# Block-sparse attention in front of a top-2 mixture of experts: dense heads in split f16 against gathered key blocks in f32

## The chip, the cores and the metric

The kernel runs on one core of one Trainium2 chip. The metric is the time of one execution in device microseconds (us); the median of several executions is given where there are several. A core has five engines with queues of their own: TensorE (PE, its weight loads shown as PEld), VectorE (DVE), ScalarE (ACT), GpSimd (POOL) and SyncE (SP), which only issues DMAs. DMAs can be issued on SP's, ACT's and POOL's queues; they share 16 DMA engines. Within a queue everything goes in order, so a DMA that has to wait holds back what stands behind it.

## The reference, cut to what matters

The attention has 4 batches, 8 heads, 768 positions and 64 columns a head. The mask is by blocks of 32: a query block sees its neighbours, the first and the last key block, and three key blocks that come as input; the first and the last query block see everything.

```python
mask = np.abs(blk_i - blk_j) <= 1
mask = mask | (blk_i == 0) | (blk_j == 0) | (blk_i == n_blocks - 1) | (blk_j == n_blocks - 1)
for qb in range(n_blocks):                       # 24 blocks
    for kb in sampled_blocks[qb]:                # 3 each, an input
        mask[qb*32:(qb+1)*32, kb*32:(kb+1)*32] = True
scores = np.where(mask, scale * q @ k.T, -1e9)
attn = softmax(scores); x = attn @ v             # then (B*S, H*D) = (3072, 512)
noisy = x @ w_gate + log1p(exp(x @ w_noise)) * noise
# each row goes to its two best of 8 experts, with softmax weights over the two:
out[row] += weight * (relu(x[row] @ w1[e]) @ w2[e])       # w1: 512x1024, w2: 1024x512
```

All inputs are f32 but the block numbers, which are 64-bit integers.

## The kernel before

The program is written in the order in which each engine's queue is to run; there is no planner behind it. It has two stages.

**Attention** goes head by head, two heads a group, in 192 steps (32 heads x 6 key tiles of 128). Q, K and V are loaded on ACT's queue. Q and K are split into an f16 high and low part (`split`, ACT and POOL), and turned by DMA transposes on SP (`xpose`). The mask rides along as 24 extra columns: one-hot block numbers times 2^15 on the query side, allowed blocks on the key side. For each step PE computes a first product only for the row maxima (`max_mm`, line 214), DVE takes the maximum over 768 columns (`max_red`, line 221), the maximum is put back into the operands by another DMA transpose (line 232), PE computes the scores transposed, keys by queries, in two f16 matmuls of 384 columns (`exp`, lines 245 and 246), ACT takes the exp out of PSUM (line 247), and PE multiplies by V in f32, two column tiles at once (`av`, line 302). The row sums are added up over key tiles by POOL or DVE, whichever a running estimate of their work says is free (`plus`, line 271), summed by PE with a matrix of ones (line 313), and the result is turned back by PE (line 341), scaled by DVE (line 344) and split into f16 high and low (lines 353, 355).

**The router** (`Router.run`) is a chain of some forty small operations for each batch. It is a generator: a call of `background` lets it go one step, between the operations of attention, and for the last batch between those of the first expert. It ends in twelve indirect DMAs on POOL that write row number and weight into a table of slots, ordered by expert.

**The experts** (`Experts`) come in nine units: expert 0 for the first three batches (unit 0, 640 slots), expert 0 for the last batch (unit 1, 224 slots), and experts 1 to 7 with 816 slots. For a unit, SP loads its slots (`meta`, line 809), POOL gathers the rows (`gather`, line 836), SP turns them by DMA transpose (`xpose`, line 846), PE runs the two layers in split f16 (`mm1` line 888, `mm2` line 908), DVE multiplies by the weight and adds what is there already (`finish`, line 949), which POOL has gathered from the output before (`gather_prev`, line 854), and POOL scatters the rows to the output (line 955). Weights come in eight pieces for each expert (`load_piece`, SP, line 792) and are split into high and low f16 by ACT and DVE (`split_piece`, lines 799 and 800).

What belongs to the seam stands in the main function: a dictionary `plan` says at which attention step the router's inputs are loaded, the output is zeroed (`fill_out`, line 1078, eight DMAs on ACT's queue from step 20 on), the first weight pieces are loaded, and slots, gathers and transposes of unit 0 are issued, in the last 14 steps.

Of the kernel before, what the change touches and what calls it, by code (L numbers as in the profile page):

```python
# [18 lines left out]
P = 128  # L19
# [18 lines left out]


class Attention:  # L40
    G = 2
    XM = 2
    RN = 5
    S0 = 4
    Q2LATE = 1
    ROWLATE = 2
    LOADAT = 2
    VLOADAT = 6

    SPLITAT = ((0, 0, 0), (1, 0, 1), (2, 1, 0), (5, 1, 1), (5, 2, None), (6, 3, None), (8, 4, None), (9, 5, None))  # L50
    PPB = 5
    STEP = 2000
    AHEAD = 4000
    SPARE = 2000
    LA = 4

    def __init__(self, tc, q, k, v, sampled):
        self.tc, self.nc = tc, tc.nc
        self.q, self.k, self.v, self.sampled = q, k, v, sampled
        self.B, self.H, self.S, self.D = q.shape  # L60
        self.T = self.S // P
        self.NB = self.S // 32
        self.LM = self.T + 5
        self.NG = self.B * self.H // self.G
        self.NSTEP = self.B * self.H * self.T
        self.st = {}
        self.todo = {}
        self.now = 0
        self.busy = {"v": 0.0, "p": 0.0, "a": 0.0}

    def open(self, ctx, early):

        tc, nc, G, T = self.tc, self.nc, self.G, self.T
        pool = lambda c, name, bufs, **kw: c.enter_context(tc.tile_pool(name=name, bufs=bufs, **kw))
        self.const = pool(ctx, "aconst", 1, side="right")
        self.tp = pool(ctx, "atp", 3, side="right")
        self.pp = pool(ctx, "app", self.PPB, side="right")
        self.sm = pool(ctx, "asm", 4, side="right")
        self.xp = pool(ctx, "axp", 2, side="right")
        self.ps_e = pool(ctx, "ps_e", 3, space=PSUM)  # L80
        self.ps_m = pool(ctx, "ps_m", 2, space=PSUM)
        self.ps_o = pool(ctx, "ps_o", 1, space=PSUM)
        self.natp = pool(ctx, "anat", 1, side="right")
        self.raw = pool(early, "araw", 2)
        self.nat = [tuple(self.natp.tile([P, G, T, P], F16, name=f"{n}{i}") for n in ("ka", "qa", "qb"))
                    for i in range(2)]
        self.k2 = [self.natp.tile([P, G, T, P], F16, name=f"k2{i}") for i in range(3)]
        self.vx = [self.natp.tile([P, G, T, self.D], F32, name=f"vx{i}") for i in range(3)]

        self.inv = self.natp.tile([P, 32], F32, name="inv")  # L90
        nc.gpsimd.memset(self.inv, 1.0 / XS)
        self.ident = self.natp.tile([P, P], F32, name="ident")

    def masks(self, mi, sb):

        nc, T, NB, G = self.nc, self.T, self.NB, self.G
        BIG = 2.0 ** 15
        bc = lambda a, n: a[:, None, :].to_broadcast([P, T, n])
        rowi = mi.tile([P, T], I32, name="rowi")
        nc.gpsimd.iota(rowi, pattern=[[1, T]], base=0, channel_multiplier=T)  # L100
        ei = mi.tile([P, NB], F32, name="ei")
        nc.gpsimd.iota(ei, pattern=[[1, NB]], base=0, channel_multiplier=0,
                       allow_small_or_imprecise_dtypes=True)
        self.kb = mi.tile([P, G, T, P], F16, name="kb")
        nc.gpsimd.memset(self.kb[:, :, :, 64:], 0.0)
        nc.gpsimd.memset(self.kb[:, :, :, 64 + NB:65 + NB], 64.0)
        self.blank(0)
        nc.vector.tensor_scalar(rowi, rowi, 5, None, op0=ALU.arith_shift_right)
        rowb = mi.tile([P, T], F32, name="rowb")
        nc.vector.tensor_copy(rowb, rowi)  # L110
        rb = rowb[:, :, None].to_broadcast([P, T, NB])
        eh = mi.tile([P, T, NB], F32, name="eh")
        nc.vector.tensor_tensor(eh, bc(ei, NB), rb, op=ALU.is_equal)
        self.eh = eh
        self.blocks(0, 1)
        t1 = mi.tile([P, T, NB], F32, name="t1")
        nc.vector.tensor_tensor(t1, bc(ei, NB), rb, op=ALU.subtract)
        al = mi.tile([P, T, NB], F32, name="al")
        nc.vector.tensor_tensor(al, t1, t1, op=ALU.mult)
        nc.vector.tensor_scalar(al, al, 1.5, None, op0=ALU.is_lt)  # L120
        e0 = mi.tile([P, NB], F32, name="e0")
        nc.vector.memset(e0, 0.0)
        nc.vector.memset(e0[:, 0:1], 1.0)
        nc.vector.memset(e0[:, NB - 1:NB], 1.0)
        nc.vector.tensor_tensor(al, al, bc(e0, NB), op=ALU.add)
        nc.vector.tensor_tensor(al, al, eh[:, :, 0:1].to_broadcast([P, T, NB]), op=ALU.add)
        nc.vector.tensor_tensor(al, al, eh[:, :, NB - 1:NB].to_broadcast([P, T, NB]), op=ALU.add)
        sbf = mi.tile([P, 3, NB], F32, name="sbf")
        nc.vector.tensor_copy(sbf.rearrange("p j e -> p e j"), sb.rearrange("p (e j) k -> p e j k", j=3)[:, :, :, 0])
        t3 = mi.tile([P, T, 3, NB], F32, name="t3")  # L130
        nc.vector.tensor_tensor(t3, sbf[:, None].to_broadcast([P, T, 3, NB]),
                                rowb[:, :, None, None].to_broadcast([P, T, 3, NB]), op=ALU.is_equal)
        for j in range(3):
            nc.vector.tensor_tensor(al, al, t3[:, :, j], op=ALU.add)
        for g in range(G):
            nc.vector.tensor_scalar(self.kb[:, g, :, 64:64 + NB], al, 0.0, -BIG, op0=ALU.is_equal, op1=ALU.mult)

    def blank(self, i):
        ka, qa, qb = self.nat[i]
        self.nc.gpsimd.memset(qa[:, :, :, 64 + self.NB:], 0.0)  # L140
        self.nc.gpsimd.memset(qb[:, :, :, 64 + self.NB:], 0.0)

    def blocks(self, i, k):
        for g in range(self.G):
            self.nc.vector.tensor_scalar(self.nat[i][k][:, g, :, 64:64 + self.NB], self.eh, 2.0 ** 15, None, op0=ALU.mult)

    def load(self, g, eng=None, names="kq"):
        b, h0 = divmod(g * self.G, self.H)
        r = self.st.setdefault(g, {})
        for nm in names:  # L150
            if nm == "v":
                x = r["v"] = self.vx[g % 3]
                (eng or self.nc.scalar).dma_start(x.rearrange("p h t d -> p h (t d)"),
                                                  self.v[b, h0:h0 + self.G].rearrange("h (p t) d -> p h (t d)", p=P))
                continue
# [5 lines left out]
    def new(self, r, nm):  # L161
        r[nm] = self.tp.tile([P, self.G, self.T, P], F16, name=nm)
        return r[nm]
# [34 lines left out]
    def where(self, n):  # L198
        hh, i = divmod(n, self.T)
        g, h = divmod(hh, self.G)  # L200
        return g, h, i
# [1030 lines left out]
```

## Time and profile before

| | us |
|---|---|
| median of 3 runs (lowest, highest) | 1067.92 (1065.22, 1068.31) |
| span of the profiled execution, first to last instruction | 1027.3 |
| attention: start to the first expert matmul | 438.3 |
| experts: from there to the last matmul's output | 572.4 |
| tail | 16.6 |
| PE busy in the span | 952.4 |
| DVE, ACT, POOL busy in the span | 506.3, 374.4, 518.5 |

The profile is of one execution. Its own time is not listed apart from its span; the median of the runs is 40.6 us above the span, which is what lies around the first and last instruction. In the rows of groups the columns are line, engine, operation, tiles written <- read, shapes and count; then the busy time of the group, the mean ns of one, the engine's idle time just before them, and what ended it. Names such as `po<-p,vx` are the program's own tile names. Matmuls overlap in the pipeline, so a group's count times its mean is more than its busy time; an f32 matmul shows as two records.

### The profile page before, as it was taken

Reading aid. Unit: us, or ns where it says so; the run is one execution under the profiler, and the core shown is the slowest. Engines: PE = TensorE matmul, PEld = TensorE weight load, DVE = VectorE, ACT = ScalarE, POOL = GpSimd, SP = SyncE. Lnnn points to the kernel's source line nnn. Section 1 sums busy time; section 2 is a strip of 40 time slices with the busy share of each in tenths; the row PEclk is TensorE's granted clock in tenths of the full one; section 3 lists DMA queues with packets and bytes.
Section 4 is the critical chain, followed back from the end, with each engine's and each line's share of the span. In section 5 each row is a group of like instructions: output and inputs, shape, how many; then the busy total and the mean of one; then the engine's idle time right before and its main releaser. Section 6 shows DMA issues by size and latency. Waiting matters only on the chain. (4 is left out here: it accounts for less than half of the span.)

```text
span 1027.3 us, 14952 instructions
## 1 busy us (share of the span) xinstructions
PE 952.4 (93%) x5633; PEld 452.3 (44%) x5633; DVE 506.3 (49%) x845; ACT 374.4 (36%) x795; POOL 518.5 (50%) x488
## 2 busy tenths in 40 slices
PE   3999999999999989789779999999999999989993
PEld 1344343444344434265545455454454544544541
DVE  6666669876887776165414425134143341341220
ACT  2566656565566645443203124032031230320200
POOL 2687886887688758925434142151342512612111
PEclk9999999999999989999889999999999999999997
DMA  8899975787577647655588539269295393681200
GB/s 193 187 183 274 250 185 112 156 163 161 128 154 153 122 100 130 134 165 122 151 219 205 185 109 257 82 159 227 73 219 156 116 220 112 152 173 56 61 34 33
DMA packets 238499, 156.04 MB, mean 152 GB/s; under 512 B 173025, under 2 KB 214241, under 8 KB 238416
## 3 DMA queue, kind: packets, MB, share of 16 engines
q1 hardware_dynamic: 207264, 91.45, 42.1%
q0 software_dynamic: 14256, 39.58, 13.3%
q10 hardware_dynamic: 16896, 23.95, 8.5%
q8 instruction: 46, 0.75, 0.3%
q14 instruction: 37, 0.30, 0.1%
HBM read 79.62 MB, written 26.32 MB: 103 GB/s over the span
## 5 line engine op out<-in xcount | busy, mean ns | idle before, releaser
L247 ACT ACTIVATE p<-pe 128x384 f32<-128x384 f32 x384 | 186.9, 491 | 154.9 <-PE pe L246 136.5
L221 DVE TENSOR_REDUCE m<-pm 128x1 f32<-128x768 f32 x192 | 182.2, 953 | 93.6 <-PE pm L214 92.1
L955 POOL DMA_INDIRECT out_dram<-y,mt x56 | 60.5, 1081 | 315.2 <-DVE y L949 211.5
L893 ACT ACTIVATE hh<-ph 128x408 f16<-128x408 f32 (+2 forms) x136 | 66.6, 490 | 340.6 <-PE ph L888 280.9
L302 PE MATMUL po<-p,vx 128*64 128x384 f32 x768 | 160.7, 511 | 0.0
L271 POOL TENSOR_TENSOR acc<-p,p 128x768 f32<-128x768 f32 x69 | 125.0, 1812 | 26.6 <-ACT p L247 26.4
L894 DVE SCALAR_TENSOR_TENSOR hl<-ph,hh 128x408 f16<-128x408 f32 (+2 forms) x136 | 76.0, 560 | 125.9 <-ACT hh L893 125.9
L245 PE MATMUL pe<-q,k 128*128 128x384 f16 x384 | 129.1, 336 | 6.5 <-DVE xr L344 3.7
L246 PE MATMUL pe<-q,k 128*128 128x384 f16 x384 | 126.5, 329 | 3.3 <-DMA q<-qb 3.3
L949 DVE SCALAR_TENSOR_TENSOR y<-py,mt,pv 128x512 f32<-128x512 f32 (+1 forms) x55 | 41.2, 749 | 168.1 <-PE py L908 150.5
L888 PE MATMUL ph<-xta,w1hb 128*128 128x408 f16 x512 | 111.2, 340 | 10.1 <-DMA xta<-xg 6.4
L908 PEld LDWEIGHTS <-hh 128*128 128x128 f16 x768 | 75.0, 98 | 98.4 <-issue 10.4
L214 PE MATMUL pm<-k,q 88*128 88x384 f16 x384 | 98.4, 341 | 18.4 <-DMA k<-kb 10.7
L888 PE MATMUL ph<-xtb,w1ha 128*128 128x408 f16 (+1 forms) x448 | 91.2, 325 | 2.9 <-DVE hl L894 2.4
L245 PEld LDWEIGHTS <-k 128*128 128x128 f16 x384 | 37.1, 97 | 118.5 <-issue 105.2
L271 POOL TENSOR_TENSOR acc<-acc 128x768 f32<-128x768 f32 x41 | 74.2, 1811 | 19.8 <-DVE acc L274 17.0
L908 PE MATMUL py<-w2ha,hh 128*128 128x512 f16 x192 | 73.8, 384 | 5.9 <-DVE y L949 5.4
L854 POOL DMA_INDIRECT pv<-out_dram,gi x56 | 57.8, 1031 | 34.5 <-issue 17.8
L908 PE MATMUL py<-w2ha,hl 128*128 128x512 f16 x192 | 73.6, 383 | 0.7 <-DVE hl L894 0.7
L908 PE MATMUL py<-w2la,hh 128*128 128x512 f16 x192 | 73.8, 384 | 0.0
L888 PEld LDWEIGHTS <-w1ha 128*128 128x128 f16 x576 | 56.4, 98 | 39.4 <-issue 3.9
L908 PE MATMUL py<-w2hb,hh 128*128 128x512 f16 x192 | 72.8, 379 | 0.4 <-DVE y L949 0.3
(179 smaller groups left out, 1306.6 us busy)
## 6 DMA issues: line engine op xcount, KB each, us to landing
wraw<-in_moe_w_dram SPq DMA_DIRECT2D x64, 512.0 KB, 5.8
q<-q SPq DMA_DIRECT2D x32, 192.0 KB, 3.3
vx<-in_v_dram ACTq DMA_DIRECT2D x16, 384.0 KB, 4.1
out_dram<-zero ACTq DMA_DIRECT2D x8, 768.0 KB, 5.2
x_rows<-x SPq DMA_DIRECT2D x16, 384.0 KB, 3.5
raw_k<-in_k_dram ACTq DMA_DIRECT2D x14, 384.0 KB, 4.1
raw_q<-in_q_dram ACTq DMA_DIRECT2D x14, 384.0 KB, 5.9
k<-k SPq DMA_DIRECT2D x17, 192.0 KB, 4.5
```

The costliest lines, as they stand in the source:

```text
L214: self.nc.tensor.matmul(pm[:, c, 0:384], r["q3"][0:K, h, t, :], r["k2"][0:K, h, 3 * c:3 * c + 3, :], start=True, stop=True)
L221: self.nc.vector.tensor_reduce(self.st[g]["m", h][:, t:t + 1], pm[:, :, 0:384], axis=AX.XY, op=ALU.max)
L245: nc.tensor.matmul(pe[:, 0:384], r["k1"][:, h, c, :], r["q1"][:, h, t, :], start=True, stop=False)
L246: nc.tensor.matmul(pe[:, 0:384], r["k2"][:, h, c, :], r["q2", h][:, t, :], start=False, stop=True)
L247: nc.scalar.activation(p32[:, t].rearrange("p t c -> p (t c)"), pe[:, 0:384], AF.Exp, scale=0.125)
L271: self.nc.gpsimd.tensor_add(out, a, b)
L302: self.nc.tensor.matmul(po[s * D:(s + 1) * D], r["v"][:, h, c, :], p32[:, 3 * s:3 * s + 3].rearrange("p t c -> p (t c)"), start=c == 0, st ...
L888: nc.tensor.matmul(ph[:, b, 0:m], w[wt][:, kb, fs], r["xt"][:, kb, a, o:o + m], start=i == 0, stop=i == last)
L893: nc.scalar.activation(hv, ph[:, b, 0:m], AF.Relu)
L894: nc.vector.scalar_tensor_tensor(self.hl[:, f, o:o + m], ph[:, b, 0:m], 0.0, hv, op0=ALU.max, op1=ALU.subtract)
L908: nc.tensor.matmul(py, h[:, f, o], w[x][:, f, :], start=i == 0, stop=i == last)
L955: nc.gpsimd.indirect_dma_start(out=self.out, out_offset=bass.IndirectOffsetOnAxis(ap=r["mt"][0:m, c, 0:1], axis=0), in_=y[0:m], in_offset= ...
```

## The change

- The host part of the launch lays Q and K out as [64 columns x 2 heads, positions] in f32 and puts the first and last query block of a batch together at the end; V gets a column of ones for each head and 32 rows of zeros at the end. So no DMA transposes and no f16 splits of Q and K, no mask columns, and no separate row sums are left in attention.
- A batch has six query tiles of 128: five of four ordinary blocks (`g` 0 to 4), and one special tile (`SPEC`) with the ordinary blocks 21 and 22 and the full blocks 0 and 23, which see all keys. Its work is 16 macros: per half of the heads D, D, X for the special tile (D: the two full blocks against 384 keys each; X: blocks 21 and 22), then G for each of the five ordinary tiles and each half.
- In a G or X, a query block has 256 key columns: 160 gathered ones (three sampled blocks, first and last block, in `KG`) and 96 that are next to each other in `KT`. POOL copies the sampled blocks of K at offsets read into registers (`gather_k`). SP loads V twice over: `VA` with the three sampled blocks, each by a DMA of its own at a register offset, and the first block; `VB` with the last block and the three neighbours (`load_v`). A sampled block that is there already, or twice, gets the zero rows of V.
- PE's score matmuls are 32 or 64 queries wide, 64 rows deep, in tiles of the array (`scores`); DVE takes the maximum from PSUM (`top`), ACT the exp (`exps`), PE turns the result in f32 (`turn`), ACT and DVE copy it out of PSUM (`evac`), PE multiplies by V and its column of ones (`av`), DVE divides (`norm`), ACT and POOL split into f16 (`high`, `low`).
- The steps run three deep: at step n the scores of macro n, the turn of n - 1, the AV of n - 2.
- Everything that attention and router load goes on SP's queue. Row stores are per tile, and the noise and row numbers follow the new order of rows (32 small DMAs for the noise).
- `fill_out` goes from attention into the first layer of unit 0, still on ACT's queue; `zero` becomes a tile of its own. Units 0 and 1 no longer read the output before they write it.
- Slots, gathers and transposes of unit 0 are issued after attention's last step, and the tiles that they write are opened there. Weight pieces 0 to 3 of expert 0 are issued in the last eight steps, as before in the last 22.
- The bookkeeping of engine work (`work`, `plus`) goes.

The diff, cut to its core:

```diff
+    def load_v(self, b, g):
+        ...
+        if self.seq(b, g) == i:
+            nc.sync.dma_start(VA[96:P], at(row, 32, [[0, 4]]))
+            nc.sync.dma_start(VB[0:32], at(row + self.S - 32, 32, [[0, 4]]))
+        ...
+        nc.sync.dma_start(VB[32:P, ks[0]:ks[0] + len(ks)], at(row + 32 * (f + ks[0] - 1), 96, [[32 * width, len(ks)]]))
+        ...
+        _, offs = nc.values_load_multi_w_load_instructions(
+            self.voff[0:1, b, 3 * f:3 * (f + n)], engines=(mybir.EngineType.SP,), min_val=0, max_val=self.ZROW,
+            skip_runtime_bounds_check_because="block numbers")
+        for j in range(n):
+            for s in range(3):
+                nc.sync.dma_start(VA[32 * s:32 * s + 32, j], v[bass.ds(offs[3 * j + s], 32)])
+    def gather_k(self, b, g):
+        ...
+        for j in range(n):
+            for s in range(3):
+                nc.gpsimd.tensor_copy(KG[:, j, :, 32 * s:32 * s + 32], KT[:, :, bass.ds(offs[3 * j + s], 32)])
+    def scores(self, m):
+        ...
+        mm = lambda out, l, r, pos: nc.tensor.matmul(out, l, r, start=True, stop=True, tile_position=pos)
+        ...
+        for some in tiles:
+            for piece in range(2):
+                for r, j, o, col in some:
+                    for a in range(2):
+                        ...
+                        mm(S[a][o:o + 32, sl], q[hp(a), pr, 32 * j:32 * j + 32], rhs, (64 * a, o))
+    def steps(self, on_tile, step):
+        ...
+        for n in range(NS + 3):
+            new, mid, old = at(n), at(n - 1), at(n - 2)
+            if old:
+                self.evac(old, 0)
+                self.evac(old, 1)
+            if new:
+                self.scores(new)
+            step(n, 0)
+            if new:
+                self.top(new)
+            if new:
+                self.exps(new)
+            step(n, 1)
+            if old:
+                self.av(old)
+                self.norm(old)
+            if mid:
+                self.turn(mid)
+            step(n, 2)
+            if old:
+                self.high(old)
+                self.low(old, on_tile)
+            if new:
+                self.ahead(n)
+            step(n, 3)
...
-        nc.vector.scalar_tensor_tensor(y[0:m], py[0:m, 0:self.D], r["mt"].bitcast(F32)[0:m, c, 1:2], self.pv[0:m, c, :],
-                                       op0=ALU.mult, op1=ALU.add)
+        if u < 2:
+            nc.vector.tensor_scalar(y[0:m], py[0:m, 0:self.D], w[0:m, c, 1:2], None, op0=ALU.mult)
+        else:
...
-    at(NS - AHEAD, ex.meta, 0)
-    for c in range(ex.count(0)):
-        at(NS - AHEAD + 2 + c // 2, gather_early, c)
-        at(NS - AHEAD + 4 + c // 2, ex.xpose, 0, c)
...
-    for i in range(8):
-        at(20 + 4 * i, fill_out, i)
+    OPEN = NS - 8
...
     att.steps(on_tile, step)
+    while not finished(B - 2):
+        background()
     late.close()
+    ex.open_left(left)
     ex.open_right(right)
+    ex.meta(0)
+    ex.indices(0)
+    for c in range(ex.count(0)):
+        ex.gather(0, c)
+    for c in range(ex.count(0)):
+        ex.xpose(0, c)
...
-    ex.gather_prev(0)
...
             if u == 0:
+                fill_out(f)
                 for i in SPLITS[f]:
                     ex.split_piece(0, i)
```

More of the change, by code (lines that the diff above doesn't have):

```diff
@@ L87, in open @@
[L87 to L136, printed above, removed]
@@ L249, in flush @@
-    def flush(self):
-        for n in sorted(self.todo):
-            for f in self.todo.pop(n):
-                f()
-    def later(self, steps, f):
-        if steps:
-            self.todo.setdefault(self.now + steps, []).append(f)
-        else:
-            f()
-    def work(self, v=0, p=0, a=0):
-        for e, x in (("v", v), ("p", p), ("a", a)):
-            self.busy[e] += x
-    def plus(self, out, a, b):
-        u, w = self.busy["v"] + 1050, self.busy["p"] + 1800
-        if out is a and min(u, w) > self.now * self.STEP - self.SPARE:
-            return False
-        if w <= u:
-            self.nc.gpsimd.tensor_add(out, a, b)
-            self.work(p=1800)
-        else:
-            self.nc.vector.tensor_add(out, a, b)
-            self.work(v=1050)
-        return True
@@ new lines, in turn @@
+    def turn(self, m):
+        kind, b, g, h, kh = m
+        p = self.st.pop(("p", m))
+        T = self.st["tp", m] = [self.ps_t.tile([P, 512], F32, name=f"t{a}") for a in range(1 if kind == "X" else 2)]
+        if kind == "D":
+            src = [(a, k, 384 * a + P * k) for a in range(2) for k in range(3)]
+        elif kind == "X":
+            src = [(0, 2 * c + u, 256 * u + P * c) for c in range(2) for u in range(2)]
+        else:
+            src = [(c, u, 256 * u + P * c) for c in range(2) for u in range(4)]
+        for t, i, o in src:
+            self.nc.tensor.transpose(T[t][:, i * P:(i + 1) * P], p[:, o:o + P], self.ident)
@@ new lines, in start, with ahead @@
+    def start(self, ip):
+        self.load_q(0, self.SPEC)
+        self.load_k(0)
+        self.index(ip)
+        self.load_vn(0)
+        make_identity(self.nc, self.ident)
+        self.gather_k(0, self.SPEC)
+        self.load_v(0, self.SPEC)
+        for g in range(2):
+            self.load_q(0, g)
+            self.load_v(0, g)
+        self.gather_k(0, 0)
+    def ahead(self, n):
+        b, i = divmod(n, self.PB)
+        order = [(bb, g) for bb in (b, b + 1) for g in (self.SPEC, *range(self.SPEC))]
+        more = b + 1 < self.B
+        last = not more
+        if i == 3 and more:
+            self.load_k(b + 1)
+        if i == 7 and more:
+            self.load_vn(b + 1)
+        unit = lambda k: order[k] if order[k][0] < self.B else None
+        qs = {6: 3, 8: 4, 10: 5, 12: 6, 14: 7} | ({0: 2} if b else {})
+        vs = {7: 3, 9: 4, 11: 5, 13: 6, 15: 7} | ({1: 2} if b else {})
+        if last:
+            vs = {7: 2, 9: 3, 11: 4, 13: 5}
+        ks = {5: 2, 7: 3, 9: 4, 11: 5, 13: 6, 15: 7}
+        for plan, f in ((ks, self.gather_k), (qs, self.load_q), (vs, self.load_v)):
+            if i in plan and (u := unit(plan[i])):
+                f(*u)
@@ L561, in run @@
         nc.vector.tensor_copy(lc, pv)
-        work(v=325)
         yield
@@ L589, in run @@
         nc.vector.reciprocal(iw, w)
-        work(v=250)
         yield
```

719 lines of the change are left out of this document (333 added, 386 removed).

## The prediction

> **What bounds the kernel now.** I read the page first (engine sums, then the groups), then three stretches of the span, then TensorE's instructions in order of time, then the queues. The first fence has the engine sums and the costly groups of attention from the page; the second has the stretches: attention, experts, tail, each row with its length and then the busy time of PE, PEld, DVE, ACT and POOL, the granted clock and the DMA share.
>
> ```profile
> PE 952.4 (93%) x5633; PEld 452.3 (44%) x5633; DVE 506.3 (49%) x845; ACT 374.4 (36%) x795; POOL 518.5 (50%) x488
> L247 ACT ACTIVATE p<-pe 128x384 f32<-128x384 f32 x384 | 186.9, 491 | 154.9 <-PE pe L246 136.5
> L221 DVE TENSOR_REDUCE m<-pm 128x1 f32<-128x768 f32 x192 | 182.2, 953 | 93.6 <-PE pm L214 92.1
> ```
>
> ```profile
> 0.00:438.30 438.30, 402.23 (x2525) 164.78 (x2525) 301.75 (x508) 245.91 (x591) 333.36 (x300) 0.99 0.76 163
> 438.30:1010.70 572.40, 550.18 (x3108) 287.56 (x3108) 203.76 (x336) 128.46 (x205) 184.12 (x187) 0.99 0.57 147
> 1010.70:1027.30 16.60, 0.00 (x0) 0.00 (x0) 0.75 (x1) 0.00 (x0) 0.98 (x1) 0.62 0.05 19
> ```
>
> PE is busy 402 of 438.3 us in attention and 550 of 572.4 in the experts, and the others wait for it (ACT 136.5 us and DVE 92.1 us of idle time end on a matmul). So attention is a PE stage. The change takes three quarters of its score work away; what counts is which resource then sets the 438.3 us, and what the seam to the experts costs. Around the span lies 1067.9 (median) - 1027.3 = 40.6 us, which I keep; the profiled execution has no time of its own listed, so the sum goes by its span and is then put on the median.
>
> **PE after the change.** f32 matmuls in column tiles, the f32 transposes and the seam, in order of time:
>
> ```profile
> 251.83 0.87 PE L302 MATMUL po<-p,vx 128*64 128x384 f32 x4
> 252.63 0.19 PE L554 MATMUL pe<-r_whl,r_xT 128*128 128x32 f16 x1
> 255.80 0.53 PE L313 MATMUL pe<-acc,inv 128*32 128x192 f32 x8
> 256.27 0.34 PE L245 MATMUL pe<-q,k 128*128 128x384 f16 x1
> 436.47 0.55 PE L341 MATMUL pe<-ident,xo 128*128 128x128 f32 x3
> 438.32 0.71 PE L888 MATMUL ph<-xta,w1ha 128*128 128x320 f16 x2 [1.30 <-DVE xr L344]
> ```
>
> Two column tiles of 384 f32 columns take 252.63 - 251.83 = 0.80 us, four of 192 take 0.47: each f32 column costs 2.1 to 2.4 ns, however many tiles share it. Transposes follow each other every (0.55 - 0.27)/2 = 0.14 us, 0.27 being the length of one. The new attention has 64 macros (16 a batch): 40 of kind G (four query blocks, four heads), 16 D, 8 X. A G has 2 x (160 + 96) = 512 score columns in eight tiles: 1.2 us; eight transposes: 1.1; AV in eight groups of four tiles of 65 columns: 1.25. That is 3.55. A pair of D: 2 x (0.8 + 6 x 0.14) + 12 x 65 x 2.4 ns = 5.2; an X: 1.8. Sum 142 + 42 + 14 = **198 us**. No row shows tiles that split the rows of the array too: if those two run one after the other, scores double and PE has about 265; if the short pieces overlap better it has 180. I take 198, since the column tiles do share.
>
> **DVE, ACT and the chain of a step.** Rows for what replaces the old work:
>
> ```profile
> L344 DVE TENSOR_TENSOR xr<-pe,rc 128x384 f32<-128x384 f32 x32 | 17.6, 549 | 2.1 <-PE pe L341 2.0
> L561 DVE COPY r_lc<-pe 128x192 f32<-128x192 f32 x3 | 1.1, 358 | 4.4 <-PE pe L556 4.4
> L949 DVE SCALAR_TENSOR_TENSOR y<-py,mt,pv 128x512 f32<-128x512 f32 x48 | 36.0, 750 | 165.4 <-PE py L908 150.5 <-DMA pv<-out_dram,gi 11.8 <-DMA slots<-r_pay,r_sl 3.1
> L336 DVE RECIPROCAL rc<-sbt 128x6 f32<-128x6 f32 x32 | 6.1, 192 | 1.1
> L274 DVE TENSOR_TENSOR acc<-p,p 128x768 f32<-128x768 f32 x27 | 28.1, 1040 | 0.0
> L274 DVE TENSOR_TENSOR acc<-acc 128x768 f32<-128x768 f32 x12 | 11.5, 955 | 0.0
> L334 DVE STREAM_TRANSPOSE sbt<-sb 128x192 f32<-128x192 f32 x32 | 11.8, 370 | 20.1 <-ACT sb L331 20.1
> L331 ACT ACTIVATE sb<-pe 128x192 f32<-128x192 f32 x32 | 10.5, 327 | 3.4 <-PE pe L313 3.4
> ```
>
> DVE in a G: two maxima over 512 (953 x 512/768 = 0.64 each), two small operations on four columns and the reciprocal (under 0.2 each), one copy of 512 out of PSUM (0.70, between 358 x 512/192 and 750), one scaling of 256 (0.37): 2.9 us. D pairs 3.3, X 1.9: 115 + 27 + 15 = 157. The maxima over 768, the sums and the rest of the old attention go. What is left of DVE's 301.75 us when the rows of lines 221, 274, 334, 336 and 344 are taken off (182.2 + 28.1 + 11.5 + 11.8 + 6.1 + 17.6), 44 us of router and start, stays: 200 us. ACT: four exps of 256 (0.38 each, from 327 for 192 and 491 for 384), a copy of 512 (0.6), half of a 512 conversion: 2.4 a G, 133 in all. Per macro the order is scores, maximum, exps, turn, evacuation, AV, spread over three steps with two score buffers: 1.2 + 1.45 + 1.5 + 1.1 = 5.25 us over two steps, so at least 2.6; PE's 3.55 is larger. With hand-overs, and the D pairs holding both score buffers until the exps, I take 4.0 a step: 64 x 4.0 = **256 us**, plus 15 for the start.
>
> **SP, the queue that gets nearly everything.** Loads that went out on ACT's queue now go on SP's, and each gathered value block is a DMA of its own, whose offset is first read into a register. First two issues in order of time, then lines with min/median/max ns of one issue; L971 is the only read of a value into a register; then the bytes of the first 438 us, all and ACT's queue.
>
> ```profile
> 1.23 0.42 SPq L368 DMA_DIRECT2D raw_k<-in_k_dram  x1
> 1.70 0.42 SPq L368 DMA_DIRECT2D raw_q<-in_q_dram  x1
> L538 SPq DMA_DIRECT2D x_rows<-x x16: 583/964/1328, 73.7 to 441.3; - x16
> L536 SPq DMA_TRANSPOSE r_xT<-x x16: 1313/1528/4252, 70.1 to 439.8; - x16
> L971 SPq TENSOR_LOAD <-o_nt x1: 472/472/472, 987.3 to 987.3; - x1
> L836 POOLq MOVE  x56: 29/29/29, 405.9 to 888.0; - x56
> DMA packets 143892, 71.54 MB, mean 163 GB/s; under 512 B 111216, under 2 KB 137328, under 8 KB 143856
> q10 hardware_dynamic: 16896, 23.95, 20.0%
> ```
>
> Counted from the code: 264 gathers (24 tiles, six of them a batch, 12 blocks each but 6 for the first); 166 other plain DMAs (8 K, 4 VN, 24 Q, 24 + 16 VB, 22 end blocks, 32 x_rows, 36 for router inputs and the table); 24 transposes; 264 register values. A plain issue repeats every 1.70 - 1.23 = 0.47 us; I take 0.5 for the 166 = 83. Transposes 24 x 1.58 = 38. A gather is a small DMA of 32 rows: 0.47 plus some register arithmetic (29 ns an instruction), 0.57, so 150; its bounds are 0.47 and the 1.01 of an average x_rows issue. A register value lies between one 472 ns load for each list of 12 (11 us in all) and 472 ns for each value (125); I take 60, the middle, because a list is one address range and most of 472 ns should be the round trip. Sum 83 + 38 + 150 + 60 = **331 us**, bounds 255 (with all low) and 512. [...] No run here shows a list yet.
>
> SP works in order. A value load waits for the AV that frees its buffer (three buffers, two in the last batch); behind it stand the next Q, the row stores and the next batch's K. The wait falls five steps before the use, so in a SP-bound stage PE is there first and it costs nothing.
>
> Bytes: the code moves 72.6 MB in attention (17.6 gathered V, about 23.4 VB and ends, 12.6 Q and K, 6.4 VN, 12.6 rows and their transposes), as much as the 71.54 before, but in runs of 2 KB. ACT's queue moved 23.95 MB of such runs in 20.0% of 438 us, 273 GB/s: 266 us, under SP's sum.
>
> **POOL.** K blocks are gathered by copies of 128 columns at a register offset:
>
> ```profile
> masks.py:199 POOL TENSOR_SCALAR_AFFINE_SELECT ident<-ident 128x128 f32<-128x128 f32 x1 | 0.3, 292 | 0.1
> L355 POOL TENSOR_TENSOR x<-xr,x 128x384 f16<-128x384 f32 x31 | 28.4, 915 | 0.2
> L716 POOL DMA_INDIRECT slots<-r_pay,r_sl x36 | 38.9, 1081 | 8.9 <-issue 5.9 <-DVE r_ot L706 2.4 <-DVE m L221 0.6
> ```
>
> 264 copies at 0.29 to 0.5 (take 0.4): 106; their values 60; 24 subtractions of 512 columns at 1.22 = 29; scatters 39; end blocks 16: 250, under SP too (172 to 342).
>
> **The seam and the experts.** First the latencies to landing (us, last number) of what fills the first expert, then min/median/max ns of an issue:
>
> ```profile
> out_dram<-zero ACTq DMA_DIRECT2D x8, 768.0 KB, 5.2
> xg<-x_rows,gi POOLq DMA_INDIRECT x56, 4.9
> xta<-xg SPq DMA_TRANSPOSE x33, 5.5
> mt<-slots SPq DMA_DIRECT2D x1, 5.0 KB, 2.8
> L809 SPq DMA_DIRECT2D mt<-slots x9: 340/530/538, 407.8 to 844.3; - x9
> L1078 ACTq DMA_DIRECT2D out_dram<-zero x8: 542/550/628, 67.4 to 123.4; - x8
> L836 POOL DMA_INDIRECT xg<-x_rows,gi x56: 923/998/1497, 411.1 to 894.5; - x56
> ```
>
> Before, slots, gathers and transposes of the first expert were issued during attention and PE idled 1.30 us. Now they follow its last step: norm, high, low about 3 us; on SP the last transpose and row store 2.6; slots 0.9 + 2.8; limits 0.4; five gathers at 1.05 on POOL, the last landing 4.9 later; its transpose 5.5: **25 us** of idle PE, 24 more than before. Loading the first weights in the last eight steps hides behind attention as before. Zeroing on ACT's queue is 8 issues of 0.55, hidden (ACT has 128 us of work in 572); its 6.3 MB meet the weights in the first unit, where the output scatters also wait for it: 5 us by estimate (0 to 20). Seven gathers of earlier output fall away on POOL, which is idle: nothing. The different DVE operation for the first two units costs the same.
>
> **Sum.** Attention is set by SP: 331, plus 5 while SP stands for the first offsets, plus about 12 from the last value load's issue to the last matmul less 8 of row work behind it: 340. First expert matmul at 365 instead of 438.3; experts 572.4 + 5; tail 16.6: span 959, and with 40.6 around it **1000 us**; the likeliest case's own range is 955 to 1045.
>
> **Rivals.**
> (1) SP is not the bound: gathers at 0.47 and lists read at once, 255 us, and then the chain of a step (256 + 15) sets attention: 271 + 25 + 577 + 17 + 41 = 931, range 905 to 955. For it: the nearest issue row; against: POOL and the DMA engines stand near 255 too.
> (2) Slower: a gathered block costs SP more than 1.06 us (issue and value together, I took 0.80). Then 264 x 0.26 = 69 us more, attention ends at 409 and the seam and zeroing eat the rest: 1068 at the turning point, 1115 at 1.24, 1180 at the upper ends (1.01 + 0.47 = 1.48). For it: x_rows at 0.96 and the only register row at 0.47; against: the 0.42 of short issues.
> (3) The clock falls. PE would be busy 198 of 340 us with gaps at each wait, and the tail's row shows 0.62 granted where PE stands still, against 0.99 in attention. At half clock for the whole stage PE has 396 us and the time is about 1055. [...]
> (4) The change doesn't shorten attention at all because the DMA engines fill: 72.6 MB at the 163 GB/s of before is 445 us, about 1110 in all. Against: that was 256-byte packets for the most part.
>
> **Chances.** Forecast 0.47, (1) 0.24, (2) 0.20, (3) 0.04, (4) 0.02, and 0.03 for an end within 0.3% of before, which is about what runs of this kernel can tell. Faster 0.75, same 0.04, slower 0.21. The range 910 to 1095 takes in (1), the forecast, (3) and the nearer part of (2), and leaves out under 2 in 10.
>
> **What would show it.** Right: attention's last matmul near 340, SP issuing back to back through it, about 0.8 us between gathers, PE busy near 200 us before the seam, 25 us of idle PE, experts within 10 us of 572. If SP shows long stands and the steps last 4 us, (1); if the gathers come every 1.1 us or more, (2); if the clock row is well under 0.9 in attention, (3). Wrong altogether would be an expert stage that grows by tens of us: PE waiting for weights or for output scatters behind the zeroing, which I priced at 5.

## The result, and the profile after

The changed kernel takes **1100.93 us** (median of 4 runs, 1097.33 to 1103.69) beside 1067.04 (1065.22 to 1068.31) for the kernel before in the same comparison: ratio **1.0317 [1.0284, 1.0351]**. I had forecast 1000 in a range of 910 to 1095. The same kernel was timed twice more beside the kernel before: 1.0247 [1.0176, 1.0317] (1058.41 us) and 1.0407 [1.0369, 1.0445] (1106.55 us). Chips differ: before takes 1033 to 1034 us in two of the five comparisons and 1064 to 1067 in three, so below only ratios, or profiles of one group of chips, are compared. I call them the quick chips (1033) and the slow chips (1066).

First the stretches of the changed kernel's profiled execution (1101.8 us, span 1100.0; slow chip): attention, seam, experts, tail; then the same two large stretches of the kernel before and of the changed kernel on quick chips. Columns: stretch, length, busy time of PE, PEld, DVE, ACT, POOL, granted clock of PE (1.00 is full), DMA share (mean busy share of the 16 DMA engines), GB/s.

```profile
0.00:456.00 456.00, 264.57 (x6761) 201.03 (x6761) 186.87 (x580) 133.62 (x310) 142.78 (x413) 0.78 0.67 166
456.00:474.60 18.60, 1.51 (x49) 1.36 (x48) 0.93 (x4) 0.63 (x1) 7.26 (x8) 0.54 0.64 155
474.60:1081.90 607.30, 560.12 (x3060) 289.49 (x3060) 204.82 (x336) 128.31 (x204) 181.03 (x178) 0.96 0.58 145
1081.90:1100.00 18.10, 0.00 (x0) 0.00 (x0) 0.75 (x1) 0.00 (x0) 0.98 (x1) 0.60 0.05 18
```

```profile
0.00:432.70 432.70, 400.54 (x2514) 164.08 (x2514) 300.39 (x505) 244.98 (x588) 330.88 (x299) 0.99 0.78 165
436.80:1012.90 576.10, 551.58 (x3108) 288.37 (x3108) 203.78 (x336) 128.20 (x205) 183.12 (x187) 0.98 0.58 146
```

```profile
0.00:439.90 439.90, 244.39 (x6758) 190.90 (x6759) 186.43 (x580) 133.95 (x310) 142.12 (x413) 0.81 0.70 172
458.50:1041.80 583.30, 553.05 (x3060) 287.24 (x3060) 204.03 (x336) 128.85 (x204) 180.97 (x178) 0.97 0.60 151
```

On quick chips the 30.0 us between the spans (1060.1 - 1030.1) are attention +7.2, seam +14.5 (18.6 for 4.1), experts +7.2 and tail +1.1. The change did what it says: PE's work in attention fell from 400.5 to 244.4 us, DVE's from 300 to 186, ACT's from 245 to 134, POOL's from 331 to 142. No engine is full any more, and yet attention isn't shorter. So the question is what each engine waits for. PE's waits in the first 456 us of the changed kernel, then those of SP's queue (us in all, times, longest):

```profile
PE pe L536 <- DMA r_xT<-x: 45.1, 6, 15.1
PE s L197 <- DMA q<-in_q_dram: 37.4, 8, 13.1
PE s L197 <- issue: 22.8, 35, 1.4
PE t L277 <- ACT p L253: 18.5, 8, 7.6
PE po L305 <- DMA va<-in_v_dram: 17.4, 11, 4.7
```

```profile
SPq L516 <- POOL x L372: 62.0, 5, 26.8
SPq L171 <- DMA vb<-in_v_dram: 12.9, 8, 3.1
SPq L144 <- PE pe L619: 12.5, 1, 12.5
```

And a batch border (where one batch's last tiles end and the next batch's scores begin) in order of time, SP's queue first, then PE:

```profile
128.76 6.23 SPq L171 DMA_DIRECT2D va<-in_v_dram  x12
135.04 0.42 SPq L144 DMA_DIRECT2D q<-in_q_dram  x1
135.57 1.29 SPq L516 DMA_TRANSPOSE r_xT<-x  x1
```

```profile
139.00 0.21 PE L536 MATMUL pe<-r_whl,r_xT 128*128 128x32 f16 x1 [14.65 <-DMA r_xT<-x]
139.52 1.56 PE L197 MATMUL s<-kt,q 64*64 64x384 f32 x8
```

The router's matmuls of a finished batch stand in PE's order ahead of the next scores. They need the last row tile's transpose; SP issues it only at 135.57, behind the twelve gathers of a value tile. PE stands 14.65 us. While PE stands no new tile is finished, and SP then stands for the next batch's first row tile, 62.0 us at five places. The two wait for each other in turn, at each of three borders. PE's second row, the wait for Q, stands on the same queue: Q too is issued behind the twelve gathers (135.04).

### The profile page after: what moved, and what is told of

Its sections match the earlier page's. It is cut to its first block, busy times and chain, and to the rows that moved or that the text cites. A ratio compares the mean times of both kernels' runs of the same rounds, so it can differ in the third digit from the quotient of the medians.

```text
span 1100.0 us, 24431 instructions
## 1 busy us (share of the span) xinstructions
PE 826.2 (75%) x9865; PEld 491.9 (45%) x9865; DVE 393.4 (36%) x921; ACT 262.6 (24%) x515; POOL 332.1 (30%) x600
## 5 line engine op out<-in xcount | busy, mean ns | idle before, releaser
L262 ACT ACTIVATE p<-s,nb 128x256 f32<-128x256 f32 x176 | 69.5, 475 | 165.2 <-DVE nb L240 77.8
L188 POOL COPY kg<-kt 128x128 f32 x264 | 64.0, 295 | 114.1 <-PE s L197 88.2
L277 PE MATMUL t<-ident,p 128*128 128x128 f32 x448 | 79.9, 328 | 23.2 <-ACT p L253 18.5
L223 DVE TENSOR_REDUCE nm<-s 128x2 f32<-128x512 f32 (+1 forms) x96 | 57.5, 641 | 111.0 <-PE s L197 102.3
L197 PE MATMUL s<-kg,q 64*32 64x160 f32 x1408 | 62.3, 360 | 46.3 <-DMA q<-in_q_dram 27.3
L197 PE MATMUL s<-kt,q 64*32 64x96 f32 (+1 forms) x1536 | 68.1, 316 | 31.4 <-issue 15.5
L305 PE MATMUL po<-va,t 128*32 128x65 f32 x1408 | 63.5, 257 | 37.0 <-DMA va<-in_v_dram 17.4
L372 POOL TENSOR_TENSOR x<-xr,x 128x512 f16<-128x512 f32 x24 | 27.8, 1157 | 184.3 <-ACT x L364 152.7
L277 PEld LDWEIGHTS t<-ident,p 128*128 128x128 f32 x448 | 60.5, 167 | 34.1 <-ACT p L253 13.2
L845 PEld LDWEIGHTS <-w1hb 128*128 128x128 f16 x512 | 50.9, 99 | 55.4 <-issue 18.7
```

Source lines behind the costliest of these rows:

```text
L188: nc.gpsimd.tensor_copy(KG[:, j, :, 32 * s:32 * s + 32], KT[:, :, bass.ds(offs[3 * j + s], 32)])
L197: mm = lambda out, l, r, pos: nc.tensor.matmul(out, l, r, start=True, stop=True, tile_position=pos)
L223: red = lambda out, x: nc.vector.tensor_reduce(out, x, axis=AX.X, op=ALU.max, negate=True)
L262: self.nc.scalar.activation(p[:, 256 * u:256 * u + 256], S[a][:, 256 * r:256 * r + 256], AF.Exp, bias=nb[:, u:u + 1], scale=0.125)
L277: self.nc.tensor.transpose(T[t][:, i * P:(i + 1) * P], p[:, o:o + P], self.ident)
L305: mm = lambda o, n, hl, l, r, start, stop: self.nc.tensor.matmul(O[o:o + n, hl], l, r, start=start, stop=stop, tile_position=(0, o))
```

## Experiments

Theories, by their letters: **A**, SP and PE wait for each other at the borders; **B**, SP's own work sets attention; **C**, the low granted clock does; **D**, PE runs out of instructions because blocks of them queue among the value transfers; **E**, PE takes instructions faster than they come, whatever else moves; **F**, the DMA engines' time on the value rows; **K**, **P**: in the version where POOL gathers, stops of PE at a low clock (K) or POOL's order (P) set the time. e0 to e3, e4 with e5 to e7, e8 to e10 and e11 to e14 were timed together.

**e0**: the kernel before once more, for a profile with its own time.

> The kernel before, unchanged, for a second profile of it. The one profile of it that the prediction used has a span of 1027.3 us, 40 below its timed runs, while the changed kernel's profile (1100.0) lies 1.8 below its own time. If what lies around the span is about 2 us in both, this profile's span will be 1063 to 1067, and the 40.6 us that the prediction kept as a constant was a difference between executions. If it really lies around the span, the span will be 1025 to 1030 again. With a span near 1065 the experts should be longer than 572 us in it (590 to 610) and attention near 450.

1031.89 us with a span of 1030.1: **1.8 us lie around the span**, not the 40.6 that I had kept. The execution whose page I read before (span 1027.3) and the timed runs (1067.92) were on chips of the two kinds.

**e1**, the router's start moved away from the border; its matmuls begin 61 instead of 13 background calls after a batch's rows are handed over:

```
-    ZN, ZL = 13, 18
+    ZN, ZL = 61, 18
```

> The changed kernel, with one number altered: the router of a batch starts its matmuls 61 background calls after its rows are handed over instead of 13 (about four steps later instead of one). Theory A (two queues wait for each other at the batch borders: PE stands at the router's matmul until SP has turned the last rows, and SP then stands until PE has gone on): the three waits of about 21 us at the borders shrink to 5 to 10, 30 to 50 us in all, 1050 to 1070. Theory B (SP's issue rate alone sets attention, the wait at the border is only SP's backlog showing there): the sum of SP stays, time within 10 us of 1101. Theory C (the low clock in attention, 0.76, sets the length of the steps): within 10 us of 1101.

1033.92 us, ratio **0.9988 [0.9957, 1.002]**: level with before, and 24 us under the changed kernel on a quick chip (e4), less than the 30 to 50 that A expected. As **e14**, beside the unchanged kernel on one slow chip:

> The changed kernel with the later router, on the same chip. Theory A (mutual wait at the batch borders costs 24 us on any chip): ratio 0.995 to 1.005, 0.024 to 0.03 under the changed kernel's. If the gain came from the chip alone, it stands level with the changed kernel.

> The changed kernel, unchanged, on the same chip as the others. On a chip with before near 1033: ratio 1.02 to 1.03, attention near 440, stops under 10 us in sum. On one with before near 1067: ratio 1.03 to 1.035, attention near 456, stops above 15 us.

0.9977 [0.9943, 1.0012] beside 1.0407 [1.0369, 1.0445]. PE's waits in e13, then in e14:

```profile
PE pe L536 <- DMA r_xT<-x: 45.4, 6, 14.4
PE s L197 <- DMA q<-in_q_dram: 35.3, 8, 13.2
```

```profile
PE pe L536 <- DMA r_xT<-x: 26.9, 4, 7.5
PE s L197 <- DMA q<-in_q_dram: 30.5, 6, 13.6
```

```profile
SPq L171 <- DMA vb<-in_v_dram: 19.6, 13, 2.8
SPq L516 <- POOL x L372: 18.4, 5, 12.2
```

Attention falls from 455.9 to 416.7 us, and SP's wait for the low halves is 18.4 us where the changed kernel has 62.0. One number in the order of issue is worth as much as the whole loss against the kernel before: e1's attention is 415.7 us beside 432.7, which pays for the longer seam and experts. A is shown as one part of the cause.

**e2** and **e3**: one transfer with fixed rows in place of the twelve gathers and their list (the values are then those of other blocks; the bytes stay); e3 with the later router too. Cut to its core:

```
-        _, offs = nc.values_load_multi_w_load_instructions(...)
-        for j in range(n):
-            for s in range(3):
-                nc.sync.dma_start(VA[32 * s:32 * s + 32, j], v[bass.ds(offs[3 * j + s], 32)])
+        nc.sync.dma_start(VA[0:96, 0:n], at(row + 32 * (f - 1), 96, [[32 * width, n]]))
```

> The changed kernel with the sampled blocks of V loaded at fixed rows: one DMA of 96 rows and all blocks of a tile instead of 12 (or 6) gathers, and no values read into registers on SP. The same bytes move; which rows they are is left out of the computation. Takes 240 issues of 0.5 us and 59 us of register reads from SP, about 175 us. Theory A and B: attention falls from 456 to the chain of the steps, 280 to 340, total 925 to 990. Theory C: steps stay as long as the clock makes them, attention over 420, total over 1065. If the DMA engines bound it (about 74 MB), attention stays over 400 too.

> Both edits together: V at fixed rows, router 61 calls later. Theory A: with SP unburdened the last rows are turned in time, so the later router adds little: 0 to 15 us below the run with V at fixed rows alone. Theory B: the same. Theory C: within 10 us of 1101.

1032.37 (0.9972 [0.9939, 1.0005]) and 1014.9 (0.9833 [0.9776, 0.9891]). Attention 404.2 and 386.5. SP's gathers and lists are thus worth 26 us of time and 36 of attention from e4 to e2, 19 and 29 from e1 to e3. A and B expected far more of e2, 925 to 990 us in all: with SP busy for 198 us of e3's attention, where it is 302 in e4's, attention still stands at 386.5 us, 46 above my forecast. B falls as the whole cause. What goes on in it is in the windows of e3, 0 to 386.5 and 100 to 200 us:

```profile
0.00:386.50 386.50, 246.25 (x6758) 192.37 (x6759) 187.13 (x580) 134.25 (x310) 142.72 (x413) 0.82 0.86 195
100.00:200.00 100.00, 65.60 (x1871) 51.38 (x1862) 50.09 (x160) 35.72 (x83) 38.28 (x104) 0.84 0.88 204
```

The DMA engines are at 0.86 of full. The row of the one queue that SP feeds (packets, MB, share of 16 engines, over 386 us):

```profile
q1 hardware_dynamic: 63458, 74.50, 84.6%
```

With the small queues that is 333 us of 16 engines' time, 194.5 of it on 22784 rows of 2080 bytes at 137 ns mean. And PE stops inside groups that wait for nothing; weight loads of e3 in order of time:

```profile
88.83 0.19 PEld L192 LDWEIGHTS s<-kg,q 64*32 64x32 f32 x8 [3.69 <-issue]
96.56 0.43 PEld L272 LDWEIGHTS t<-ident,p 128*128 128x128 f32 x4 [3.25 <-issue]
102.34 0.15 PEld L300 LDWEIGHTS po<-vb,t 128*32 128x32 f32 x5 [1.92 <-issue]
```

These are PE's records 2241, 2497 and 2753 of the trace: 256 apart, as are nearly all such stops, in whatever line. e3's attention has 53 such borders of 256 records; PE stops for over 0.3 us at 22 of them, and is idle 65.5 us at all of them in sum. In the changed kernel it is 17.6 (35.2 on a quick chip); that its waits for SP take the place of the others is my reading. The DMA queue q8, which the profile calls `instruction`, moves packets of 16384 bytes: 53 in the first 386 us of e3, 53 in the 456 us of the changed kernel's attention and 20 in the 438 us of before's, in each about one for 256 of PE's records (53 borders, 13,693 records, 5,080 records). That PE stops there because such a packet comes late is my reading; no trace shows which packet a stop waits for.

**e5**, the right rows of V and the later router, half the gathers on ACT's queue with reads of their own (the call is cut):

```
+        for eng, kind, js in ((nc.sync, mybir.EngineType.SP, range(0, n, 2)), (nc.scalar, mybir.EngineType.Activation, range(1, n, 2))):
+            for j in js:
+                _, offs = ...(self.voff[0:1, b, 3 * (f + j):3 * (f + j) + 3], engines=(kind,), ...)
+                for s in range(3):
+                    eng.dma_start(VA[32 * s:32 * s + 32, j], v[bass.ds(offs[s], 32)])
```

> The changed kernel with the router 61 calls later, and the gathers of V shared by two queues: blocks 0 and 2 of a tile on SP, 1 and 3 on ACT, each with its own reads of the offsets. Takes about 130 x 0.5 + 30 = 95 us from SP. If SP's issue is all that is left between the router-later run and the fixed-V run, it comes to their combination or a little above, 1005 to 1025, ratio to before 0.975 to 0.99. If the reads of offsets on ACT hold up its exps as much as SP is relieved, it stays at 1030 to 1045.

1047.33, 1.0155 [1.006, 1.0249], 13 us above e1 by medians and 2 above the upper end that I gave for the case that ACT is held up. PE's first wait, ACT's, and one such wait in order of time:

```profile
PE po L306 <- ACT t L289: 98.8, 22, 11.3
```

```profile
ACT t L289 <- DMA va<-in_v_dram: 89.9, 17, 8.5
```

```profile
154.69 3.59 ACTq L172 DMA_DIRECT2D va<-in_v_dram  x6
158.32 0.60 ACT L289 ACTIVATE t<-t 128x512 f32<-128x512 f32 x1 [3.72 <-DMA va<-in_v_dram]
```

The evacuation that PE needs (L289) stands in ACT's order behind the gathers. In the stretch shown ACT doesn't wait for a buffer: it issues six gathers back to back, and reads a list of three offsets (0.71 us) between the third and the fourth. Of the 89.9 us, 53 are instructions of this kind; the rest are the short gaps between them and waits. So mainly SP's issue work went to a queue that has urgent work.

**e4**, the changed kernel again, with **e6** (e3, but batches 1 to 3 load neither gathered nor neighbouring blocks of V; the plain load of V for the special tile, `VN`, stays) and **e7** (e3, with the second AV product of the G macros left out and all transfers kept):

```
 e6     def load_v(self, b, g):
+           if b:
+               return
 e7 -           for c, V in enumerate((VA, VB)):
    +           for c, V in enumerate((VA,)):
    ...
```

> The changed kernel, unchanged, timed beside the three experiments of this call, so that differences are read on one chip. The ratio to before should be 1.025 to 1.037 again; with before near 1034 that is 1060 to 1072.

> V at fixed rows and router later, and the gathered and neighbouring blocks of V loaded in batch 0 alone; batches 1 to 3 multiply by what batch 0 left, so their values are left out. Instructions of PE are the same; about 30 MB of 74 in attention go. Theory D (PE runs out of instructions every 256, because their loads queue among the V loads): the gaps at multiples of 256 go in batches 1 to 3 and stay in batch 0; a batch takes 65 to 75 us instead of 88 to 95, the whole 930 to 965. Theory E (PE takes instructions faster than they can be fetched, whatever else moves): the gaps stay, only waits for V go, 985 to 1005. Theory C (the low clock sets the steps): 995 to 1015.

> V at fixed rows and router later, with the second of the two AV products of each ordinary tile left out (the last and the neighbouring key blocks don't count). The DMA traffic is the same, PE has 5120 fewer instructions in attention of some 13600. Theory D and E: fewer blocks of 256, the gaps fall by a third to a half of about 95 us: 965 to 985. If the bytes themselves (waits for V) set the pace, attention stays within 8 us of the run with both edits, 1000 to 1020.

1058.41 (1.0247 [1.0176, 1.0317]), 938.11 (0.9087 [0.9006, 0.9168]), 974.92 (0.9442 [0.9364, 0.952]). Batches 0 to 3 of e6; only the first loads these blocks:

```profile
28.12:124.44 96.32, 58.27 (x1649) 45.30 (x1648) 40.34 (x104) 32.43 (x75) 25.53 (x80) 0.79 0.71 165
124.44:192.74 68.30, 53.39 (x1703) 42.12 (x1703) 47.48 (x151) 33.23 (x78) 38.24 (x104) 0.95 0.54 119
192.74:259.43 66.69, 52.74 (x1704) 41.55 (x1703) 47.75 (x151) 33.01 (x78) 38.06 (x104) 0.95 0.50 117
259.43:320.90 61.47, 46.22 (x1546) 38.71 (x1547) 42.44 (x134) 29.45 (x69) 30.95 (x77) 0.89 0.44 93
```

A batch without these transfers takes 67 to 68 us, 4.2 a step, at a granted clock of 0.95; batch 0 with them 96, at 0.79, and in e3 batches 1 and 2 take 89 and 90, at 0.85 and 0.83, with the same work. C, which expected 995 to 1015, falls: the clock isn't what holds the steps by itself, it rises when the transfers go. The stops at the borders of 256 fall too, from 65.5 to 32.3 us in sum; in batches 1 and 2 from 44.1 to 10.3. So most of them come with the transfers (D), not with the rate of PE alone (E); they don't go altogether, as D expected. In e7 attention falls by 24.5 us, PE's busy time by 25.3 (246.3 to 221.0), and the DMA share rises to 0.92 for the same 333 us of engine time. If the bytes alone had set the pace, attention would have stayed within 8 us. So the engines' time doesn't hold e3 alone: PE's slowed work and its waits add up. The time of e7 fits D and E alike, and tells them apart no further.

**e8**, the right rows of V, the later router, and the gathers on POOL: one indirect transfer (an address for each row is read from a list) of 96 rows for each query block, no list on SP. **e9**: the changed kernel, zeroing put back into steps 20 to 48. **e10**: e3 with 1040 of each 2080 bytes in batches 1 to 3. Cut to the core:

```
 e8 +            nc.gpsimd.indirect_dma_start(out=VA[0:96, j], out_offset=None, in_=v[0:nr],
    +                in_offset=bass.IndirectOffsetOnAxis(ap=self.voff[0:96, b, f + j:f + j + 1], axis=0), ...)
 e9 +    for i in range(8):
    +        at(20 + 4 * i, fill_out, i)
    -                fill_out(f)
 e10+        h = width // 2 if b else width
    ...
```

> The changed kernel with the router spread over more steps, and the 264 gathers of value blocks and their 24 register lists taken off SP: POOL gathers the 96 rows of a query block by one indirect transfer with a list of rows on 96 partitions, 92 such transfers in all. The computation is the full one. Theory F (with SP free, the DMA engines set attention: with the fixed rows they were busy 333 of 386.5 us, with the same bytes as here): 1005 to 1030 us beside 1033 for the kernel before, attention 385 to 400, DMA share about 0.85, and this would be a version that beats both. Theory A (SP and the router wait for each other) asks the same. Rival P (POOL becomes the ordered queue: 92 issues of about 1.0 us, behind which the K copies and the low halves stand while a transfer waits for its buffer): 1035 to 1070, with scores waiting for kg.

> The changed kernel with one part undone: the eight zeroing transfers of the output go out on ACT's queue in steps 20 to 48 of attention, as before the change, instead of during the first expert. If zeroing beside the first weights costs the experts what they grew by (583 us beside 576 in the kernel before on this chip), the experts fall by 5 to 10 us; if attention has room for 6.3 MB (its DMA share is 0.70 while SP stands), attention keeps its 440 us and the time is 1048 to 1054 beside 1058. If the DMA engines set attention (theory F), 6.3 MB more cost it 15 to 27 us there and the time is 1063 to 1078. My prediction's price for the move was 5 us.

> The kernel with fixed value rows and the later router, where batches 1 to 3 load only the first 260 of 520 columns of each value row; the rest of each buffer keeps older values. The number of transfers, rows and instructions is the same, 1040 bytes a row instead of 2080. Theory F (bytes through the DMA engines): the value rows' 194 us of engine time fall by some 60 to 70, attention from 386.5 to 325 to 345, the time 950 to 975. Theory D (instruction blocks queue behind value transfers) gives a part of it, 980 to 1000, if what counts is the number of packets in the queue. If the number of transfers or of waits set it: 1005 to 1020.

On a slow chip: e8 1069.96 (1.0024 [0.9988, 1.0061]), e9 1114.62 (1.0456 [1.0408, 1.0503]), e10 999.8 (0.9358 [0.9324, 0.9392]). e10 has the transfers, rows and instructions of e3 (0.9833) and gains 0.0475, some 50 us: bytes count, as F said. Its attention, 352.1 us on this chip, lies above F's 325 to 345. e8's ratio lies at the lower edge of P (1035 beside 1033), but PE waited only 7.2 us for K copies there. e9's experts take 606.8 us beside 607.3 in the changed kernel, so zeroing cost the experts nothing; its attention is 463.6 beside 456.0. The 7.6 us lie between nothing and F's 15 to 27. By the ratios zeroing in the experts is no loss (1.0456 beside 1.0317 and 1.0407).

**e11** is e8 again, **e12** e8 with the low halves on DVE.

> The kernel in which POOL gathers the value rows by indirect transfers, router later, once more, beside the changed kernel and the later router on the same chip. Theory K (what it lost on the first chip are stops of TensorE at a low granted clock, 53 us of them in attention): on a chip with few stops attention falls from 433 to 375 to 395 us and the ratio to before from 1.002 to 0.975 to 0.985. Theory P (POOL's order holds it, whatever the clock): attention stays at 415 to 430 and the ratio at 0.995 to 1.005. If the chip is again one with before near 1067, the stops return, and the ratio stays near 1.00.

> The same as e11 with the 24 subtractions for the low halves on DVE instead of POOL, which stood 104 us for ACT's conversions in them with K copies and value gathers behind. Theory P: attention 10 to 25 us shorter than in e11. Theory K or F (clock, or bytes through the DMA engines): within 5 us of e11, since TensorE seldom waits for POOL there (7 us for kg).

Again a slow chip: 1.0063 [1.0027, 1.01] and 1.014 [1.0051, 1.0228]; attention 427.0 and 440.0. Taking the low halves off POOL gained nothing, where P expected 10 to 25 us. What a gather costs POOL, in e8's attention:

```profile
L174 POOL DMA_INDIRECT va<-in_v_dram,voff x88 | 87.0, 989 | 23.6 <-issue 21.8 <-PE t L283 0.9 <-DMA x_rows<-x 0.3
```

Stops of PE of 0.2 to 1.1 us that end on nothing the profile shows sum to 47.5 us in e11's attention, 19.0 in e13, 21.9 in e14, and 6.8 in e4 on a quick chip. They come in beats (shown in the last section), and mostly while POOL issues indirect transfers: 69 of e11's 94 stops fall into the 121 us of attention in which it does so, 25 of e13's 40 into 35 us. So on this chip POOL's gathers brought stops of PE with them (47.5 us beside e14's 21.9). K tied the stops to a low clock, and the traces don't bear this out: 44 of the 94 begin at half clock, which holds for 160 of the 386 us that the clock's record covers. Whether POOL's gathers would win on a quick chip stays open: no quick chip ran them. No version that computes everything beat the kernel before; e1, one constant, is level with it.

## Why the prediction was wrong

**The sum's base.** "With 40.6 around it" was a false term: 1.8 us lie around the span. Without it the sum is 961 where before takes 1030, and the ratio 0.93 stays what I forecast; the error was the size of attention, not this.

**Attention is set by SP: 331 plus 9.** The terms of SP hold; the changed kernel's rows (min/median/max ns):

```profile
L166 SPq TENSOR_LOAD <-voff x24: 1277/2500/3212, 11.2 to 438.9; - x24
L171 SPq FUSED_REGOPS  x264: 2/37/702, 12.7 to 448.4; - x132
L171 SPq MOVE va<-in_v_dram x264: 3/29/693, 12.8 to 448.4; - x132
L171 SPq DMA_DIRECT2D va<-in_v_dram x264: 3/316/1822, 12.9 to 448.5; - x132
L516 SPq DMA_TRANSPOSE r_xT<-x x24: 1238/1274/2395, 61.8 to 458.8; - x24
```

A list of twelve takes 2500 ns, 208 a value: 58.8 us in all for my 60. That most of a single load's 472 ns is a round trip was my estimate; the runs show only the two lengths, 472 ns for one value and 2500 for twelve. A gather repeats every 0.5 us (6.23 / 12 in the row of 128.76) for my 0.57, a transpose takes 1.27 for 1.58. SP's instructions take about 307 us, 350 with the short gaps between them, for my 331; beside that it stands for about 107. Two steps failed. **The first step that failed** is the sentence that SP's waits cost nothing because "in a SP-bound stage PE is there first". I followed the value loads' wait and not the other one on that queue: the transposes of row tiles, which the router's matmuls need and which stand behind the value loads. e1 and e14 price it at 24 (1058.41 to 1033.92 on two quick chips) and 45 us (1106.55 to 1061.68 on one slow chip).

**"273 GB/s: 266 us, under SP's sum"** is **the second step that failed**. The engines needed 304 us in the changed kernel and 333 in e3, for 75.6 MB where I had counted 72.6. ACT's queue, my source for the rate, moved packets of 1536 bytes for the most part, not runs of 2 KB. Rows of 2080 bytes take 129 to 137 ns where my rate gives 122 (2080 x 16 / 273). The larger miss is a term that I didn't price apart: the transposes of the row tiles move in packets of 256 bytes, and their 6 MB take 42 us of engine time in the changed kernel and 57 in e3, where my rate gives 22. Nor is the engines' time hidden under SP's sum: e6 gains 66 us of attention by fewer bytes where SP has no gathers. I listed full DMA engines as rival (4) with 0.02, at the rate of before. They don't hold the changed kernel alone (share 0.67 to 0.70), nor e3 (0.86) quite alone (e7), but most of what I missed comes with these transfers: half the bytes of three batches gave some 50 us, none of them 77.

**PE: 198 us at 0.99.** 264.6 us at a granted 0.78 (244.4 at 0.81 on a quick chip). The sum was right, the 0.99 was not: the clock's record has only full and half (30 stretches of each in the changed kernel's profile). In e4's attention 88.8 of PE's 244.4 busy us fall into stretches at half clock; taking half of them as the clock's price (an estimate) leaves 200. A transpose repeats every 0.11 us at full clock and 0.21 at half; my 0.14 was the mean of two repeats in one group, of 0.17 and 0.11. So rival (3), 0.04, came true in part. What brings the half clock on was not shown: gaps of 15 us are there at the borders, but of 22 stretches at half clock in e4's attention, 9 begin after 7 us in which PE was never idle for more than 3.1 us at once. What the clock costs the whole stage, beside PE's own work, was not isolated.

**The chain of a step** came out close: "I take 4.0", and 4.2 is what e6 shows once the value transfers are gone.

**Seam and experts.** 14.5 us more for 24 forecast; experts 7.2 more for 5 (quick chips), and e9 shows that it isn't the zeroing, which I had blamed. The rest of it was not followed up.

So on quick chips attention's 440 us against 340 are: some 36 to 53 for SP's gathers and lists and the borders together (e2, e3), 66 for three batches of value transfers (386.5 to 320.9 from e3 to e6), in which the stops at borders of 256 records and the lower clock are contained; and e6's 321 lies under my 340, since SP no longer counts there. Rival (2), a dearer gather, was not the cause: a gather with its value costs SP 0.71 us, less than the 0.80 I took.

## What to carry to other kernels

When several kinds of work share one in-order queue, follow each kind to the engine that waits for it, above all the ones issued last in a round: here the 24 transposes behind the 264 gathers cost as much (24 to 45 us) as the gathers and their lists (19 to 36). When a change takes much of the arithmetic away, sum the transfers' engine time first, each size of packet at its own price (here 29 ns for 256 bytes and 129 for 2080 in the changed kernel), because bytes that didn't shrink may be the next bound. An order of issue tuned for the old lengths (a constant like 13 here) has to be set again before such a change is judged.

## What the hardware showed that I had not expected

- PE stopped at borders of 256 records with the DMA engines at 0.86: 65.5 us over 53 borders in e3, none over 20 in the kernel before, whose PE takes 5,080 records in attention where the changed kernel's takes 13,693.
- On slow chips PE stops in a beat of 0.7 us in some stretches. In the changed kernel, score matmuls in order of time:

```profile
160.38 0.32 PE L197 MATMUL s<-kt,q 64*32 64x96 f32 x3 [1.06 <-issue]
161.11 0.31 PE L197 MATMUL s<-kt,q 64*32 64x96 f32 x1 [0.40 <-issue]
161.81 0.58 PE L197 MATMUL s<-kt,q 64*32 64x96 f32 x8 [0.39 <-issue]
```

  0.73 and 0.70 us from start to start, with about 0.4 of it idle. Windows on both sides of the point where the clock falls to half:

```profile
156.20:160.60 4.40, 1.86 (x19) 0.80 (x15) 0.00 (x0) 1.23 (x4) 3.73 (x7) 1.00 0.05 8
160.70:167.40 6.70, 5.90 (x126) 4.35 (x128) 3.37 (x10) 2.58 (x6) 1.15 (x1) 0.50 0.02 3
```

  Most of the stops here fall into the first window, at full clock. POOL issues indirect transfers in it (the router's writes to the table of slots); 24 of the changed kernel's 39 such stops in attention fall into the 35 us in which POOL does this. On a quick chip (e1) as many such transfers have none. Why only slow chips stop there is open.
- The kernel before differs by 3% between chips (1033 and 1066 us), while runs of a kernel on one chip mostly lie within 1.6%.
